# A beacon attention with an expert layer behind it: one sequence's values loaded as plain fp32 on another queue, and cast on VectorE

## The chip, the cores and the metric

The kernel runs on one core of a Trainium2 chip. The core has TensorE (PE) for matrix products, VectorE (DVE), ScalarE (ACT) and GpSimd (POOL) for everything else, and SyncE (SP), which here only issues transfers. Sixteen DMA engines move data between the chip's memory and the core's on-chip memory; GpSimd's transfers go through a queue of its own (q0 in the profile, its descriptors written by software), SyncE's through another (q1, hardware). Each engine runs its own list of instructions in order and waits on semaphores for the others. The metric is the device time of one execution in microseconds; a lower one is better.

## What is computed

Eight sequences (B = 8) of 576 tokens with 8 heads of 64 go through causal attention, with 16 beacon keys and values that every token sees; then all 4608 tokens go through an expert layer with a leaky ReLU.

```python
k_all = np.concatenate([beacon_k, k], axis=2)
v_all = np.concatenate([beacon_v, v], axis=2)
scores = scale * np.matmul(q, k_all.transpose(0, 1, 3, 2))
scores = np.where(causal, -1000000000.0, scores)
a = np.exp(scores - scores.max(-1, keepdims=True))
a /= a.sum(-1, keepdims=True) + 1e-09
x = np.matmul(a, v_all).transpose(0, 2, 1, 3).reshape(B * S, H * D)
h = x @ w_in                              # 512 -> 2048
return np.maximum(0.01 * h, h) @ w_out    # 2048 -> 512
```

## The kernel before

Heads go in pairs g: four pairs for each sequence, 32 in all, so pairs 0 to 3 are the first sequence and 4 to 7 the second. For each pair the queries and keys are loaded, turned so that the head's 64 numbers lie on partitions, multiplied to score tiles in PSUM, taken through the exponential by ScalarE into aT, masked along the diagonal by GpSimd (L285), and multiplied with the values (L355). The values of a sequence lie in one of two buffers v_aug (bf16), in five chunks of 128 key rows (the last has 80; the first begins with the 16 beacon rows), with a column of ones that gives the sum for the normalisation on VectorE (L384, L385). The result is turned into xT, over which the expert layer runs in chunks of 512 tokens: 16 first steps to a chunk (moe1, L438, with ScalarE's leaky ReLU into a tile gT, L446), and then second steps (moe2, L514). The gT tiles come from a pool of two buffers, so a chunk's tile takes the place of that of two chunks before.

The order of all engines is written out by hand. For the first two sequences it is the string HEAD, a list of steps that are recorded one after another; each engine runs its own part of a step in that order. The letters that matter here: `l6.0` and `l6.1` load queries and keys of pair 6 (load_qk, L158); `q6` and `k6` turn them (t_q, L239) and copy them out of PSUM (L245; the number behind the dot names the copying engine: 0 VectorE, 1 ScalarE, 2 GpSimd, and none means 0); `s6.0` is the first of pair 6's four score tiles, `m6.0` the first of its three masks; `v4.0` and `v4.1` are the halves of pair 4's product with the values; `x1` turns pair 1's result; `u` is one first step of the expert layer, `d` one second step; `i0`, `i1` load the halves of w_in (L131), `o0`, `o1` those of w_out (L137), `L` beacon keys (L181); `N8.0`, `N8.1` and `T8` load and turn pair 8, the third sequence's first, with transposing transfers on SyncE's queue; `V1.3` loads chunk 3 of the second sequence's values.

A value load is made by load_v_cast, L199 to L213: GpSimd issues it (L205 for the beacon rows, L210 for the rest), and the transfer casts fp32 to bf16 on its way, straight into v_aug. Chunk 0 takes two transfers, so V1.0 to V1.4 are six. GpSimd's other loads stand in the same list and go through the same queue, between its masks. Semaphores for its transfers are reused by eights: a ninth transfer is issued when the first has landed.

Of the kernel before, what the change touches and what calls it, by code (L numbers as in the profile page):

```python
# [8 lines left out]
FP32 = mybir.dt.float32  # L9
BF16 = mybir.dt.bfloat16  # L10
# [5 lines left out]
def kernel(  # L16
# [21 lines left out]
    NF = DF // 128  # L38
# [41 lines left out]
    gpool = ctx.enter_context(tc.tile_pool(name="gpool", bufs=2))  # L80
# [21 lines left out]
    v_bufs = [singles.tile([128, NKB, H, D + 1], BF16, name=f"v_aug{i}") for i in range(2)]  # L102
# [98 lines left out]
    def load_v_cast(b, c):  # L201
        dst = v_bufs[b % 2]
        lo = 0
        if c == 0:
            nc.gpsimd.dma_start(  # L205
                out=dst[0:NB, 0, :, 0:D], in_=beacon_v[b].rearrange("h p d -> p h d")
            )
            lo = NB
        n = ROWS[c] - lo
        nc.gpsimd.dma_start(  # L210
            out=dst[lo : ROWS[c], c, :, 0:D],
            in_=v[b, :, OFF[c] : OFF[c] + n].rearrange("h p d -> p h d"),
        )  # L213
# [38 lines left out]
    def score(g, n):  # L252
        qT, kT = qk[g]
        if n == 0:
            probs[g] = a_bufs[g % NA]
        aT = probs[g]
        parts = SCORES[n]
        sc = ps_sc.tile([128, 2, 512], FP32, name="sc", tag="sc")
        c0 = parts[0][3]
        for c, q0, w, col in parts:  # L260
            for par in range(2):
                ps_ = slice(par * 64, par * 64 + 64)
                nc.tensor.matmul(  # L263
                    out=sc[:, par, col - c0 : col - c0 + w],
                    lhsT=kT[ps_, c * 128 : (c + 1) * 128],
                    rhs=qT[ps_, q0 : q0 + w],
                    start=True,
                    stop=True,
                    skip_group_check=True,
                )  # L270
        w = sum(p[2] for p in parts)
        nc.scalar.activation(  # L272
            out=aT[:, :, c0 : c0 + w], in_=sc[:, :, 0:w], func=AF.Exp, scale=0.125
        )
# [150 lines left out]
    gT = {}  # L425
# [425 lines left out]
    HEAD = "F0 F1 K Z I l0.0 l1.0 J O l1.1 l2.0 l2.1 V0.0 V0.1 l3.0 l3.1 V0.2 V0.3 V0.4 l4.0 l4.1 i0 P w13.256 C B w13 h0.1 h1.0 q0.1 k0 w2.384 s0.0 m0.0 w3.256 s0.1 q1 s0.2 m0.1 k1 s0.3 m0.2 w2.384 s1.0 m1.0 q2 s1.1 k2 w2.384 s1.2 m1.1 w2.384 s1.3 m1.2 W0.0.4 s2.0 m2.0 W0.0.4 s2.1 W0.0.6 q3 l5.0 l5.1 s2.2 k3 w4.384 v0.0 m2.1 s2.3 i1 m2.2 W0.1.4 s3.0 m3.0 v1.0 s3.1 v0.1 s3.2 v1.1 m3.1 l6.0 l6.1 s3.3 x0.1 m3.2 v2.0 V1.0 V1.1 q4 v2.1 x1 k4.1 v3.0 v3.1 x2.1 s4.0 s4.1 x3 m4.0 V1.2 V1.3 V1.4 l7.0 l7.1 u u s4.2 s4.3 q5 k5 m4.1 m4.2 u o0 u L s5.0 s5.1 m5.0 u u u s5.2 s5.3 q6 k6 m5.1 m5.2 o1 u u s6.0 s6.1 m6.0 u v4.0 u v4.1 s6.3 s6.2 q7.0 k7.0 v5.0 u N8.0 m6.1 v6.0 u s7.0 s7.3 m6.2 N8.1 v6.1 N9.0 v5.1 y4 c u s7.1 x5.0 t0 x6.0 m7.0 s7.2 u m7.1 D u v7.0 m7.2 v7.1 d t1 N9.1 d x7.1 b9.2 d b10.2 T8 t2 N10.0 V2.0 d t3 N10.1 d T9 d b8.2 V2.1 b11.2 T10"  # L851
    NG = B * NPAIR
    KEPT, LEAD, LEFT = 4, 4, 14

# [3 lines left out]
    dve, act, pool = nc.vector.tensor_copy, nc.scalar.copy, nc.gpsimd.tensor_copy  # L858
# [12 lines left out]
    def run(steps):  # L871
        for step in steps.split():
            op, a = step[0], [int(x) for x in step[1:].split(".")] if step[1:] else []
            if op == "s":
                score(*a)
            elif op == "m":
                mask(*a)
            elif op == "v":
                value(*a)
            elif op == "e":  # L880
                value_ahead(*a)
            elif op == "x":
                finish(*a)
            elif op == "l":
                load_qk(*a)
            elif op == "V":
                load_v_cast(*a)
            elif op == "N":
                load_natural(*a)
            elif op == "T":  # L890
                turn_pair(a[0])
            elif op == "y":
                x_turn(a[0])
            elif op == "q" or op == "k":
                t_q(a[0], 0 if op == "q" else 1, (dve, act)[a[1] if len(a) > 1 else 0])
            elif op == "b":
                beacon_columns(a[0], (dve, act, pool)[a[1]])
            elif op == "u":
                up()
            elif op == "d":  # L900
                down()
            elif op == "w":
                unused(*a)
            elif op == "W":
                unused_ahead(*a)
            elif op == "i":
                load_w_in(a[0])
            elif op == "o":
                load_w_out(a[0])
            elif op == "t":  # L910
                weight_sums(a[0])
            elif op == "F":
                nc.sync.dma_start(out=first_k[a[0]], in_=k[0, a[0]].rearrange("(p i) d -> p i d", i=RI))
            elif op == "K":
                load_beacon_k(0, 2, nc.scalar)
            elif op == "Z":
                nc.vector.memset(blank, 0.0)
            elif op == "I":
                nc.vector.memset(ident, 0.0)
            elif op == "J":  # L920
                make_identity(nc, ident, nomemset=True)
            elif op == "O":
                make_ones()
            elif op == "P":
                make_pads()
            elif op == "C":
                cast_beacon_k(0, 2, nc.scalar.copy)
            elif op == "B":
                beacon_transposes(0, 2)
            elif op == "h":  # L930
                (dve, act)[a[1]](out=k_nat0[:, :, a[0]], in_=first_k[a[0]])
# [18 lines left out]
    )  # L950
    with order:
        run(HEAD)

        FIRST = 2 * NPAIR
# [100 lines left out]
```

## Time and profile before

| | |
|---|---|
| median of 3 runs | 325.67 us (323.86 to 328.58) |
| the profiled execution, its own time | 323.3 us |
| its span, first to last instruction | 321.4 us |
| granted TensorE clock | 1.000 |
| DMA packets, all queues | 155769, of which 142368 under 512 B |
| queue q0 (GpSimd) | 99824 packets, 18.54 MB |
| queue q1 (SyncE) | 55632 packets, 20.62 MB |
| values, 128 rows of 8 heads, issue to landing | 6.1 us (median) |

The profile is of one execution; times within it count from the start of its span. A row of the order of time gives start, duration, engine, line, operation, tiles, and in brackets how long the engine was idle before it and what ended that. A row of a line's own answer gives the count, the shortest, median and longest duration in ns, and the first and last start; "DMA to landing" is the time from an issue to the last byte's signal. The DMA rows give packets, MB and the time that the packets took as a share of 16 engines; where packets overlap the share is over 100%.

### The profile page before, as it was taken

How to read it: one execution, taken by the hardware profiler on the slowest of the kernel's cores; microseconds unless marked ns; L12 is line 12 of the kernel's file. 1: busy time of each engine (PE TensorE's matmuls, PEld its weight loads, DVE VectorE, ACT ScalarE, POOL GpSimd, SP SyncE). 2: the span in 40 equal slices, each digit the busy share in tenths (PEclk: the TensorE clock that was granted, in tenths of full speed). 3: DMA queues.
4: the chain of work that ended last, by engine and by line, in shares of the span. 5: the costliest groups of instructions: out<-in, count | busy, mean ns of one | idle time of the engine just before them, and what ended most of it. 6: DMA issues, size and time to landing. Idle time of an engine off the chain costs nothing.

```text
span 321.4 us, 8809 instructions
## 1 busy us (share of the span) xinstructions
PE 312.5 (97%) x3518; PEld 223.5 (70%) x3542; DVE 172.7 (54%) x351; ACT 205.2 (64%) x349; POOL 186.2 (58%) x354
## 2 busy tenths in 40 slices
PE   7999999899999999999999999999999999999995
PEld 4574568565687558845888888656865687688784
DVE  3473379714455145434552454435464699577954
ACT  3978973389756786478647864787468446455510
POOL 8994989999998687659875977665221000000000
PEclk9999999999999999999999999999999999999999
DMA  8999999999999999999999999999212101200213
GB/s 134 146 200 181 146 214 131 155 197 188 151 159 183 180 143 124 132 151 118 125 171 192 126 113 124 181 139 119 64 53 87 24 0 35 88 13 1 68 63 132
DMA packets 155769, 39.79 MB, mean 124 GB/s; under 512 B 142368, under 2 KB 153504, under 8 KB 155728
## 3 DMA queue, kind: packets, MB, share of 16 engines
q0 software_dynamic: 99824, 18.54, 85.5%
q1 hardware_dynamic: 55632, 20.62, 36.9%
q8 instruction: 27, 0.44, 0.7%
q14 instruction: 14, 0.11, 0.2%
q10 hardware_dynamic: 272, 0.07, 0.1%
HBM read 37.22 MB, written 9.44 MB: 145 GB/s over the span
## 4 chain that ended last, share of the span: by engine, by line
PE 92%; ACT 4%; issue 2%; DMA 1%; DVE 0%; ACTq 0%; POOLq 0%
PE acc L438 31%; PE acc L514 23%; PE sc L514 11%; PE av L355 9%; PE sc L310 6%; PE acc L667 5%; PE sc L263 2%; ACT aT L329 2%; PE tp L239 2%; DMA gsum<-in_q_dram 1%; PE av L835 1%; ACT aT L325 1%; PE tp L401 1%; ACT gT L446 1%; ACT aT L272 1%
## 5 line engine op out<-in xcount | busy, mean ns | idle before, releaser
L438 PE MATMUL acc<-xT,w_in_sb 128*128 128x512 bf16 (+1 forms) x536 | 116.5, 354 | 1.3
L446 ACT ACTIVATE gT<-acc 128x512 bf16<-128x512 f32 x124 | 70.7, 627 | 32.0 <-PE acc L438 31.8
L285 POOL TENSOR_SCALAR_AFFINE_SELECT aT<-aT 128x256 bf16<-128x256 bf16 (+2 forms) x160 | 60.3, 406 | 51.8 <-ACT aT L325 30.5
L438 PEld LDWEIGHTS <-w_in_sb 128*128 128x128 bf16 x560 | 51.6, 98 | 42.9 <-issue 2.9
L514 PEld LDWEIGHTS <-gT 128*128 128x128 bf16 x576 | 55.0, 98 | 9.3 <-issue 1.6
L329 ACT ACTIVATE aT<-sc 128x1024 bf16<-128x1024 f32 (+3 forms) x64 | 51.8, 894 | 0.0
L384 DVE RECIPROCAL rec<-av 128x6 f32<-128x6 f32 (+1 forms) x64 | 11.9, 186 | 65.5 <-PE av L355 65.0
L514 PEld LDWEIGHTS <-gsum 128*128 128x128 bf16 x432 | 41.0, 98 | 7.3 <-issue 0.6
L325 ACT ACTIVATE aT<-sc 128x512 bf16<-128x512 f32 (+3 forms) x64 | 29.0, 521 | 25.8 <-PE sc L310 25.8
L355 PEld LDWEIGHTS <-aT 128*128 128x128 bf16 (+1 forms) x960 | 36.5, 98 | 8.0 <-issue 0.6
L355 PE MATMUL av<-v_aug,aT 128*128 128x65 bf16 (+1 forms) x960 | 38.9, 194 | 0.0
L210 POOL DMA_DIRECT2D v_aug<-in_v_dram x40 | 34.1, 859 | 3.5 <-DMA w_in_sb<-in_moe_w_in_dram 3.5
L167 POOL DMA_DIRECT2D k_nat<-in_k_dram x48 | 34.7, 729 | 1.5 <-DMA w_out_sb<-in_moe_w_out_dram 0.8
L514 PE MATMUL acc<-w_out_sb,gT 128*128 128x256 bf16 x288 | 34.6, 273 | 0.7 <-ACT gT L446 0.7
L167 POOL DMA_DIRECT2D q_nat<-in_q_dram x48 | 34.7, 728 | 0.5 <-issue 0.3
L385 DVE TENSOR_TENSOR x_nat<-av,rec 128x384 bf16<-128x384 f32 (+1 forms) x64 | 31.4, 490 | 2.4 <-DVE rec L384 0.3
L272 ACT ACTIVATE aT<-sc 128x1024 bf16<-128x1024 f32 (+3 forms) x32 | 25.9, 875 | 1.9 <-PE sc L263 1.8
L514 PE MATMUL acc<-w_sum,gsum 128*128 128x256 bf16 x192 | 23.8, 273 | 0.0
L310 PE MATMUL sc<-qT,kT 64*128 64x80 bf16 (+22 forms) x384 | 22.0, 250 | 1.5 <-issue 1.3
L789 DVE TENSOR_TENSOR gsum<-gT 128x1024 bf16<-128x1024 bf16 x18 | 12.6, 701 | 16.4 <-ACT gT L446 16.4
L310 PEld LDWEIGHTS <-kT 64*128 64x128 bf16 x384 | 12.8, 94 | 11.8 <-issue 8.8
L545 ACT COPY p<-acc 128x512 f32<-128x512 f32 x15 | 9.1, 604 | 15.7 <-PE acc L514 15.7
(95 smaller groups left out, 330.8 us busy)
## 6 DMA issues: line engine op xcount, KB each, us to landing
out_dram<-p SPq DMA_DIRECT2D x26, 256.0 KB, 3.6
q_nat<-in_q_dram POOLq DMA_DIRECT2D x48, 72.0 KB, 5.4
k_nat<-in_k_dram POOLq DMA_DIRECT2D x48, 72.0 KB, 5.4
v_aug<-in_v_dram POOLq DMA_DIRECT2D x24, 128.0 KB, 6.1
w_in_sb<-in_moe_w_in_dram POOLq DMA_DIRECT2D x2, 1024.0 KB, 12.5
w_out_sb<-in_moe_w_out_dram POOLq DMA_DIRECT2D x2, 1024.0 KB, 10.2
out_dram<-u SPq DMA_DIRECT2D x8, 256.0 KB, 3.5
gsum<-in_q_dram POOLq DMA_DIRECT2D x8, 144.0 KB, 5.6
```

The costliest lines, as they stand in the source:

```text
L167: nc.gpsimd.dma_start(out=t[:, :, par], in_=(q, k)[which][b, 2 * hp + par].rearrange("(t p) d -> p t d", p=NR),)
L210: nc.gpsimd.dma_start(out=dst[lo : ROWS[c], c, :, 0:D], in_=v[b, :, OFF[c] : OFF[c] + n].rearrange("h p d -> p h d"),)
L272: nc.scalar.activation(out=aT[:, :, c0 : c0 + w], in_=sc[:, :, 0:w], func=AF.Exp, scale=0.125)
L285: nc.gpsimd.affine_select(out=view, in_=view, compare_op=ALU.is_ge, fill=0.0, base=128 - n if lo == 0 else 0, channel_multiplier=-1, patte ...
L310: nc.tensor.matmul(out=(sc[par] if apart else sc[:, par])[:, at : at + b - a], lhsT=kT[ps_, c * 128 : (c + 1) * 128], rhs=qT[ps_, q0 : q0 ...
L325: nc.scalar.activation(out=probs[g][:, par, lo:hi], in_=sc[par][:, at : at + hi - lo], func=AF.Exp, scale=0.125)
L329: nc.scalar.activation(out=probs[g][:, :, lo:hi], in_=sc[:, :, at : at + hi - lo], func=AF.Exp, scale=0.125)
L355: nc.tensor.matmul(out=avv[:, n, 0 : D + 1], lhsT=aT[0 : ROWS[c], par, a0 : a0 + 128], rhs=va[0 : ROWS[c], c, 2 * hp + par, :], start=(c = ...
L385: nc.vector.tensor_tensor(out=x_nat[:, t0:t1].rearrange("p t e d -> p (t e) d"), in0=avv[:, :, 0:D], in1=rec[:, n0:n1, None].to_broadcast( ...
L438: nc.tensor.matmul(out=acc[:, lo:hi], lhsT=w_in_cols(fc, j), rhs=xT[:, j, x0 : x0 + hi - lo], start=(j == 0), stop=(j == NJ - 1), skip_gro ...
L446: nc.scalar.activation(out=gT[i][:, fc, :], in_=acc, func=AF.Prelu, alpha=0.01)
L514: nc.tensor.matmul(out=acc[:, lo : lo + HD], lhsT=left(i, n, fc, tile), rhs=right(n, fc), start=(lo == 0 and fc == 0), stop=(fc == HF - 1) ...
```

## The change

The second sequence's values go another way. Three functions are new and HEAD is rewritten from its 85th step on.

```diff
+    staged = []
+
+    def stage(b, c):
+        if not staged:
+            t = gpool.tile([128, NF, 512], BF16, name="gT")
+            staged.append(t.rearrange("p (s a) t -> p s (a t)", a=2).bitcast(FP32))
+        return staged[0][:, (NKB * b + c) % 8].rearrange("p (h d) -> p h d", d=D)
+
+    def load_v_plain(b, c):
+        dst = stage(b, c)
+        lo = 0
+        if c == 0:
+            nc.sync.dma_start(out=dst[0:NB], in_=beacon_v[b].rearrange("h p d -> p h d"))
+            lo = NB
+        n = ROWS[c] - lo
+        nc.sync.dma_start(
+            out=dst[lo : ROWS[c]], in_=v[b, :, OFF[c] : OFF[c] + n].rearrange("h p d -> p h d")
+        )
+
+    def cast_v(b, c, copy):
+        copy(out=v_bufs[b % 2][0 : ROWS[c], c, :, 0:D], in_=stage(b, c)[0 : ROWS[c]])
+
+    def hold_v(b, c):
+        nc.vector.memset(stage(b, c)[:, 0, 0:1], 0.0)
...
             elif op == "V":
-                load_v_cast(*a)
+                (load_v_plain if a[0] == 1 else load_v_cast)(*a)
+            elif op == "G":
+                cast_v(a[0], a[1], (dve, act, pool)[a[2]])
+            elif op == "z":
+                hold_v(*a)
```

V1.0 to V1.4 now issue plain fp32 transfers from SyncE into a tile of the gT pool, which no chunk uses yet; the first chunk's gT then takes the pool's second buffer, and chunk 1 the one with the values, once they are cast. A new step z1.0 writes one column of the staging tile on VectorE; since the first transfer overwrites part of it, that transfer waits for the write, and the others stand behind it on SyncE. Five new steps G1.0 to G1.4 cast a chunk from the tile into v_aug on VectorE. All other values (V0, V2 and on) go as before. The steps of HEAD are the same otherwise, except that some copies out of PSUM change their engine; from the 85th on, up to the first product with the second sequence's values, they stand in this order, first before and then after:

```
v2.0 V1.0 V1.1 q4 v2.1 x1 k4.1 v3.0 v3.1 x2.1 s4.0 s4.1 x3 m4.0 V1.2 V1.3 V1.4 l7.0 l7.1 u u s4.2 s4.3 q5 k5 m4.1 m4.2 u o0 u L s5.0 s5.1 m5.0 u u u s5.2 s5.3 q6 k6 m5.1 m5.2 o1 u u s6.0 s6.1 m6.0 u v4.0

v2.0 q4.0 k4.1 v2.1 z1.0 m3.2 v3.0 V1.0 x1.1 v3.1 x2.1 s4.0 s4.1 x3 k5.0 q5.0 V1.2 m4.0 u V1.3 s4.3 s4.2 l7.0 l7.1 G1.0.0 u m4.1 u L o0 m4.2 V1.1 s5.0 s5.1 u u u o1 V1.4 s5.2 G1.2.0 q6.0 G1.1.0 k6.1 u m5.0 s5.3 u m5.1 G1.3.0 s6.0 N8.0 s6.1 m5.2 G1.4.0 u v4.0
```

SyncE's list at its start, before (gsum is the staging of the first pair's keys, xT the expert layer's input, qT and kT of pairs 8 and on):

```order
L913 DMA gsum_95<-in_k_dram 64x576
L913 DMA gsum_96<-in_k_dram 64x576
L413 DMA_TRANSPOSE xT<-x_nat 128x4x128
L421 DMA_TRANSPOSE xT<-x_nat 128x112
L175 DMA_TRANSPOSE qT<-q_nat 128x6x96
L175 DMA_TRANSPOSE kT<-k_nat 128x6x96
```

The same list after:

```order
L942 DMA gsum_95<-in_k_dram 64x576
L942 DMA gsum_96<-in_k_dram 64x576
L227 DMA gT<-in_beacon_v_dram 16x8x64
L230 DMA gT<-in_v_dram 112x8x64
L230 DMA gT<-in_v_dram 128x8x64 x3
L230 DMA gT<-in_v_dram 80x8x64
L438 DMA_TRANSPOSE xT<-x_nat 128x4x128
L446 DMA_TRANSPOSE xT<-x_nat 128x112
```

Six loads stand ahead of the first transposes there. GpSimd's list before, from the load of pair 6 (gsum_547, its first rows) to that of w_out:

```order
L158 DMA gsum_548<-in_k_dram 64x2x576
L285 AFFINE_SELECT aT_93<-aT_93 128x2x128
L285 AFFINE_SELECT aT_93<-aT_93 80x2x80
L205 DMA v_aug_89<-in_beacon_v_dram 16x8x64
L210 DMA v_aug_89<-in_v_dram 112x8x64
L210 DMA v_aug_89<-in_v_dram 128x8x64
L285 AFFINE_SELECT aT_90<-aT_90 128x2x112
L210 DMA v_aug_89<-in_v_dram 128x8x64 x2
L210 DMA v_aug_89<-in_v_dram 80x8x64
L158 DMA gsum_547<-in_q_dram 64x2x576
L158 DMA gsum_548<-in_k_dram 64x2x576
L285 AFFINE_SELECT aT_90<-aT_90 128x2x128 x3
```

After (the second gsum_547 and gsum_548 are pair 7, aT_90 is pair 4's probabilities):

```order
L158 DMA gsum_548<-in_k_dram 64x2x576
L310 AFFINE_SELECT aT_93<-aT_93 128x2x128
L310 AFFINE_SELECT aT_93<-aT_93 80x2x80
L310 AFFINE_SELECT aT_90<-aT_90 128x2x112
L158 DMA gsum_547<-in_q_dram 64x2x576
L158 DMA gsum_548<-in_k_dram 64x2x576
L310 AFFINE_SELECT aT_90<-aT_90 128x2x128 x2
L181 DMA bk_raw<-in_beacon_k_dram 128x6x64
L137 DMA w_out_sb<-in_moe_w_out_dram 128x4x1024
L310 AFFINE_SELECT aT_90<-aT_90 128x2x128
L310 AFFINE_SELECT aT_90<-aT_90 80x2x80
L137 DMA w_out_sb<-in_moe_w_out_dram 128x4x1024
```

The six value loads are gone; pair 7, the beacon keys and both halves of w_out have moved ahead of masks. VectorE's list before, around the copies of qT and kT for pairs 5 and 6:

```order
L406 COPY xT<-tp 128x576
L245 COPY qT<-tp 128x576
L245 COPY kT<-tp 128x576
L245 COPY qT<-tp 128x576
L245 COPY kT<-tp 128x576
L384 RECIPROCAL rec<-av 128x6
L385 TENSOR_TENSOR x_nat<-av,rec 128x384
```

After:

```order
L431 COPY xT<-tp 128x576
L270 COPY kT<-tp 128x576
L270 COPY qT<-tp 128x576
L235 CAST v_aug_89<-gT 128x8x64 x2
L270 COPY qT<-tp 128x576
L235 CAST v_aug_89<-gT 128x8x64 x2
L235 CAST v_aug_89<-gT 80x8x64
L409 RECIPROCAL rec<-av 128x6
L410 TENSOR_TENSOR x_nat<-av,rec 128x384
```

Two casts (chunks 0 and 2) stand ahead of the copy of pair 6's qT, and three (chunks 1, 3 and 4) behind it, ahead of v4.0's normalisation; pair 6's kT has gone to ScalarE. The transfers on SyncE stand in the order of chunks 0, 2, 3, 1, 4.

More of the change, by code (lines that the diff above doesn't have):

```diff
@@ L849, in unused_ahead @@
             )
-    HEAD = "F0 F1 K Z I l0.0 l1.0 J O l1.1 l2.0 l2.1 V0.0 V0.1 l3.0 l3.1 V0.2 V0.3 V0.4 l4.0 l4.1 i0 P w13.256 C B w13 h0.1 h1.0 q0.1 k0 w2.384 s0.0 m0.0 w3.256 s0.1 q1 s0.2 m0.1 k1 s0.3 m0.2 w2.384 s1.0 m1.0 q2 s1.1 k2 w2.384 s1.2 m1.1 w2.384 s1.3 m1.2 W0.0.4 s2.0 m2.0 W0.0.4 s2.1 W0.0.6 q3 l5.0 l5.1 s2.2 k3 w4.384 v0.0 m2.1 s2.3 i1 m2.2 W0.1.4 s3.0 m3.0 v1.0 s3.1 v0.1 s3.2 v1.1 m3.1 l6.0 l6.1 s3.3 x0.1 m3.2 v2.0 V1.0 V1.1 q4 v2.1 x1 k4.1 v3.0 v3.1 x2.1 s4.0 s4.1 x3 m4.0 V1.2 V1.3 V1.4 l7.0 l7.1 u u s4.2 s4.3 q5 k5 m4.1 m4.2 u o0 u L s5.0 s5.1 m5.0 u u u s5.2 s5.3 q6 k6 m5.1 m5.2 o1 u u s6.0 s6.1 m6.0 u v4.0 u v4.1 s6.3 s6.2 q7.0 k7.0 v5.0 u N8.0 m6.1 v6.0 u s7.0 s7.3 m6.2 N8.1 v6.1 N9.0 v5.1 y4 c u s7.1 x5.0 t0 x6.0 m7.0 s7.2 u m7.1 D u v7.0 m7.2 v7.1 d t1 N9.1 d x7.1 b9.2 d b10.2 T8 t2 N10.0 V2.0 d t3 N10.1 d T9 d b8.2 V2.1 b11.2 T10"
+    HEAD = "F0 F1 K Z I l0.0 l1.0 J O l1.1 l2.0 l2.1 V0.0 V0.1 l3.0 l3.1 V0.2 V0.3 V0.4 l4.0 l4.1 i0 P w13.256 C B w13 h0.1 h1.0 q0.1 k0 w2.384 s0.0 m0.0 w3.256 s0.1 q1 s0.2 m0.1 k1 s0.3 m0.2 w2.384 s1.0 m1.0 q2 s1.1 k2 w2.384 s1.2 m1.1 w2.384 s1.3 m1.2 W0.0.4 s2.0 m2.0 W0.0.4 s2.1 W0.0.6 q3 l5.0 l5.1 s2.2 k3 w4.384 v0.0 m2.1 s2.3 i1 m2.2 W0.1.4 s3.0 m3.0 v1.0 s3.1 v0.1 s3.2 v1.1 m3.1 l6.0 l6.1 s3.3 x0.1 v2.0 q4.0 k4.1 v2.1 z1.0 m3.2 v3.0 V1.0 x1.1 v3.1 x2.1 s4.0 s4.1 x3 k5.0 q5.0 V1.2 m4.0 u V1.3 s4.3 s4.2 l7.0 l7.1 G1.0.0 u m4.1 u L o0 m4.2 V1.1 s5.0 s5.1 u u u o1 V1.4 s5.2 G1.2.0 q6.0 G1.1.0 k6.1 u m5.0 s5.3 u m5.1 G1.3.0 s6.0 N8.0 s6.1 m5.2 G1.4.0 u v4.0 q7.0 m6.0 s6.2 v4.1 u y4 N8.1 s6.3 k7.1 m6.1 v5.0 u s7.0 s7.3 m6.2 v6.0 c N9.0 u v6.1 t0 m7.0 s7.2 s7.1 u v5.1 x6.1 m7.2 u m7.1 D u v7.0 T8 v7.1 V2.0 b10.2 N10.0 x5.1 b9.2 u t1 d d t2 N9.1 N10.1 x7.1 d T9 t3 b8.2 d T10 d b11.2 V2.1 d"
     NG = B * NPAIR
```

## The prediction

> **What bounds the kernel now.** I read the page first: shares of the engines, the DMA row, the chain that ended last, the queues.
>
> ```profile
> span 321.4 us, 8809 instructions
> PE 312.5 (97%) x3518; PEld 223.5 (70%) x3542; DVE 172.7 (54%) x351; ACT 205.2 (64%) x349; POOL 186.2 (58%) x354
> DMA  8999999999999999999999999999212101200213
> q10 hardware_dynamic: 272, 0.07, 0.1%
> PE 92%; ACT 4%; issue 2%; DMA 1%; DVE 0%; ACTq 0%; POOLq 0%
> gsum<-in_k_dram POOLq DMA_DIRECT2D x7, 144.0 KB, 5.9
> bk_raw<-in_beacon_k_dram ACTq DMA_DIRECT2D x1, 64.0 KB, 2.3
> ```
>
> TensorE is busy for 97% and carries 92% of the chain, so the time can fall only where TensorE waits: 321.4 - 312.5 = 8.9 us in all. But the DMA engines are full as well, from the second slice to the twenty-eighth, and the change is one to the DMAs. Next, TensorE's order of time around the change:
>
> ```profile
> 33.95 0.76 PE L239 MATMUL tp<-ident,gsum 64*64 64x64 bf16 x36
> 36.48 0.58 PE L263 MATMUL sc<-qT,kT 64*128 64x512 bf16 x4
> 36.99 1.04 PE L438 MATMUL acc<-xT,w_in_sb 128*128 128x512 bf16 x4
> 37.87 0.53 PE L355 MATMUL av<-v_aug,aT 128*128 128x65 bf16 x12
> 60.79 0.85 PE L310 MATMUL sc<-qT,kT 64*128 64x512 bf16 x12 [1.25 <-issue]
> ```
>
> 33.95 is the turning of pair 6's queries and keys, 36.48 its first two score tiles (s6.0, s6.1), 37.87 the first product with the second sequence's values (v4.0), and 60.79 the first tile of the third sequence, with the only wait of weight in this stretch, 1.25 us. That wait is about all that the change can win. Now GpSimd, which issues the loads, and their landings:
>
> ```profile
> 18.76 0.76 POOL L131 DMA_DIRECT2D w_in_sb<-in_moe_w_in_dram  x1
> 22.12 0.61 POOL L158 DMA_DIRECT2D gsum<-in_k_dram  x1
> 23.89 1.73 POOL L210 DMA_DIRECT2D v_aug<-in_v_dram  x2
> 26.43 0.38 POOL L285 TENSOR_SCALAR_AFFINE_SELECT aT<-aT 128x224 bf16<-128x224 bf16 x1 [0.81 <-ACT aT L272]
> 31.99 0.73 POOL L210 DMA_DIRECT2D v_aug<-in_v_dram  x1 [3.45 <-DMA w_in_sb<-in_moe_w_in_dram]
> 35.46 0.78 POOL L137 DMA_DIRECT2D w_out_sb<-in_moe_w_out_dram  x1
> 38.76 0.77 POOL L137 DMA_DIRECT2D w_out_sb<-in_moe_w_out_dram  x1
> ...
> L131 POOL DMA_DIRECT2D w_in_sb<-in_moe_w_in_dram x2: 764/770/776, 12.4 to 18.8; - x2
> DMA to landing us min/median/max: 12.0/12.5/12.9
> ...
> L158 POOL DMA_DIRECT2D gsum<-in_k_dram x1: 607/607/607, 22.1 to 22.1; - x1
> DMA to landing us min/median/max: 10.9/11.0/11.1
> ...
> L210 POOL DMA_DIRECT2D v_aug<-in_v_dram x5: 730/883/905, 23.9 to 32.0; - x5
> DMA to landing us min/median/max: 5.9/10.0/10.7
> ...
> L137 POOL DMA_DIRECT2D w_out_sb<-in_moe_w_out_dram x2: 769/772/776, 35.5 to 38.8; - x2
> DMA to landing us min/median/max: 8.5/10.2/12.0
> ```
>
> The reader is to see one queue that serves in order and never runs dry: second half of w_in down at 18.76 + 12.9 = 31.7, pair 6 at 22.12 + 11.1 = 33.2, the last values at 31.99 + 5.9 = 37.9, second half of w_out at 38.76 + 12.0 = 50.8. The values took 37.9 - 33.2 = 4.7 us of it.
>
> **How two queues share the engines.** The change puts the values on SyncE's queue (q1) beside GpSimd's (q0). Four stretches of the DMA view, in order 39 to 42 us, 44.5 to 48.5, 68.5 to 69.5 and 215 to 215.5:
>
> ```profile
> q0 software_dynamic: 304, 0.62, 111.6%
> ...
> q0 software_dynamic: 347, 0.71, 95.0%
> q1 hardware_dynamic: 319, 0.08, 15.9%
> ...
> q1 hardware_dynamic: 259, 0.25, 88.5%
> q0 software_dynamic: 258, 0.03, 49.3%
> ...
> q1 hardware_dynamic: 500, 0.12, 132.6%
> ```
>
> Columns are packets, MB, share of time. Alone, w_out moves 304/3 = 101 packets a us, of 2 KB each. Against it, a transpose on q1 gets one small packet (0.08 MB/319, 256 B) for each large one: 319 against 347, some 80 a us. Turned round, 1 KB stores of q1 against 128 B packets of q0 give 259 against 258. Alone, q1 moves 500 packets in 0.5 us, 1000 a us. So the queues take turns packet by packet, whatever the size, and 256 B packets beside 2 KB ones get a twelfth of the rate that they have alone.
>
> **The change, part by part.** The values become 592 rows x 8 heads = 4736 runs of 256 B. The nearest row for a plain load of such runs by a hardware queue is that of the beacon keys above: 64 KB in 272 packets (q10), so 256 B each. I take 4736 packets.
>
> ```profile
> DMA packets 3857, 1.39 MB, mean 173 GB/s; under 512 B 3271, under 2 KB 3531, under 8 KB 3856
> 23.29 0.42 DVE L385 TENSOR_TENSOR x_nat<-av,rec 128x256 bf16<-128x256 f32 x1
> 34.47 0.76 DVE L245 COPY qT<-tp 128x576 bf16<-128x576 bf16 x1 [4.69 <-PE tp L239]
> L931 DVE CAST k_nat<-gsum x1: 745/745/745, 5.9 to 5.9; 64x576 bf16<-64x576 f32 x1
> L913 SPq DMA_DIRECT2D gsum<-in_k_dram x2: 571/573/575, 0.8 to 1.4; - x2
> 40.53 1.37 SPq L413 DMA_TRANSPOSE xT<-x_nat  x1
> ```
>
> Start: the holding write comes after value 2.1's product on VectorE, so at 23.3 + 0.4 = 23.7; six issues of 0.57 us follow, and packets flow from about 25. Behind them on SyncE stands the first transpose, issued at 40.53 before: covered unless the values are still in the ring.
>
> What q0 still holds then: the first row above is 25 to 33 us before. 3856 - 3531 = 325 packets of w_in are left, 3531 - 3271 = 260 of pair 6. Pair 7 is as large (144 KB, 256 packets), and the two halves of w_out are 2 x 512. That is 1865, with the beacon keys' 192 KB some 1900. With the values gone from GpSimd, nothing holds q0 up: pair 7's two loads follow the select of 26.43, then come two selects, the beacon keys and w_out, at about 30 to 31 instead of 35.46, before pair 6 is down. So q0 has large packets all the way.
>
> When those end: before at 50.8; less the 4.7 us of values, 46.1; plus the turns of q1. 325 + 1024 packets at 87 a us (347/4) instead of 101 cost 2.1 us, the 516 of the pairs about 0.6: 48.8. By then q1 has had some 1900 packets. The second cast needs 128 + 896 + 1024 = 2048 of them: about 49.0. The fourth needs 4096, and pair 8's queries (2 x 576 packets of 128 B) now take turns: 4096 - 1900 + 1152 at about 1000 a us, 3.4 us: 52.2.
>
> What waits: VectorE runs in order, and two casts stand ahead of its copy of qT for pair 6. 49.0 + 0.75 (cast, at the nearest row, L931) + 0.76 (copy) puts s6.0 at 50.5. Both kernels run eight expert steps ahead of it, so TensorE is there at 36.5: a wait of 14.0 us. s6.0, s6.1 and a step take 1.4 us (36.48 to 37.87), so TensorE stands at v4.0 at 51.9; the fourth cast ends at 52.2 + 0.75 = 52.95: 1.1 us more. Delay at v4.0: 52.95 - 37.87 = 15.1.
>
> Off the path: six issues of 0.5 to 0.9 us and the wait of 3.45 leave GpSimd, won nothing for TensorE but the earlier loads. Five casts, 3.7 us, lie in VectorE's idle time (4.69 us ahead of 34.47 alone); without the late data they cost nothing. Copies moved to ScalarE lie in the waits named. The swapped gT buffers cost nothing: chunk 1 is first written seventeen expert steps in, after the casts. The 1.25 us at 60.79 goes, since TensorE comes there 14 us later and pair 8 is down.
>
> Sum: 321.4 + 15.1 - 1.25 = 335.3 of span; the profiled execution had 323.3 us with 1.9 around its span, so 337.2. It lay 2.4 under the median of the runs, 325.67; between 337.2 and 339.6 I take 338.5. Bounds: data for the second cast in 46 instead of 49 changes little, since the fourth decides; that one in 49 to 55 gives 334 to 342.
>
> The Trainium skill's page "TensorE: Matmul & The Clock Gate" (part 1) adds to this: after an idle window of about 3.4 us the array runs at half rate until about 3.4 us of work have passed. By that page the sum would be an estimated 1.7 us more, 340.2. No row here shows an idle spell that long in mid-kernel, and the sum leaves it out.
>
> **Rivals.**
> (a) No slowing: the runs travel in bundles. If a packet of q1 carried 16 runs, 4 KB, 296 packets would do, and 296 turns against w_in last 296/101 + 4736/1000 = 7.6 us: values down at 32.7, before their casts. But those 4.7 us come before pair 6, down at 37.9 instead of 33.2; its turning stood at 33.95, so TensorE waits 4.0: 325.67 + 4.0 - 1.25 = 328.4, not slower by 2%; if the turning has room, 324.4. It decides from about four runs a packet: 4 x 1184 covers the values by the middle of w_out's first half. Against it stands the row of q10, one run a packet. The Trainium skill, "DMA: Bandwidth & Descriptors" (Queues, rings and completion order), has the engine take turns at packet granularity, with 9 to 17 descriptors typical of a packet. By that the bundle is likely; the trace agrees on the turns, and its 256 B packets on hardware queues speak against the bundle.
> (b) w_out comes late, because selects hold GpSimd. From pair 7's landing, near 34, q1 would run alone at 1000 a us; if w_out were 4 us later, the remaining 3900 packets would be done at 38, and v4.0 would wait 1 us: 325.67 + 1 - 1.25 = 325.4. Against it: only the masks of pair 4 stand ahead of w_out's first half now.
> (c) A won wait and no more: the load is hidden, 325.67 - 1.25 = 324.4. Since that is under 2%, faster by over 2% has hardly a mechanism.
>
> **How the numbers follow.** Forecast as worked out, 333 to 342.5: 0.70. Slower by less, 328.5 to 333, if q1 gets more turns: 0.05. (a) 0.15, (b) 0.05, (c) 0.05. About 2% is what a measurement of this kernel can tell from no change, 332.2 here: slower 0.72, same 0.27, faster 0.01. The range that holds 8 in 10 reaches from the forecast into (a), 326 to 342.5.
>
> **What would show it.** Right: q1 beside q0 near one to one from 25 to 48 us; the first cast near 36 and the second near 49; VectorE idle ahead of a cast with the transfers as releaser; TensorE idle ahead of s6.0 and v4.0, 15 us together; after that the old rhythm. Wrong: values down before 36, q1 packets above 256 B, w_out issued after 34, or a wait at pair 6's turning instead.

## The result, and the profile after

The changed kernel takes 339.4 us (median of 4 runs, 337.68 to 340.9) against 324.76 us for the kernel before, run beside it: a ratio of 1.0462, with a 95% interval of 1.0385 to 1.0539. A second set gave 340.16 us and 1.0467 (1.0391 to 1.0543). Here and below a ratio leaves disturbed executions out, so it can differ a little from that of the medians. The profiled execution took 340.9 us. Its page, from the top:

```profile
span 338.5 us, 8842 instructions
...
PE 318.2 (94%) x3542; PEld 225.0 (66%) x3542; DVE 173.0 (51%) x352; ACT 208.4 (62%) x354; POOL 182.6 (54%) x348
...
PE   7999238999999999999999999999999999999995
...
PEclk9999755999999999999999999999999999999999
...
q0 software_dynamic: 94992, 17.93, 75.0%
q1 hardware_dynamic: 60464, 21.84, 36.5%
...
PE 79%; DMA 10%; ACT 4%; SPq 3%; DVE 1%; issue 1%; POOL 1%; ACTq 0%
```

The span is 17.1 us longer. TensorE's slices 5 and 6, of 8.5 us each, hold a hole that was not there before, and in slices 5 to 7 the granted clock falls to a half. 4832 packets have moved from q0 to q1 (99824 - 94992 = 60464 - 55632): 4736 for the runs of 256 B, and 96 of 4 B, sixteen for each of the six transfers. So a run is one packet, on either queue. Transfers, which carried 1% of the chain that ended last, carry 10%. TensorE's longest waits, in us in total, times and longest:

```profile
PE sc L288 <- DVE qT L270: 9.7, 1, 9.7
PE av L380 <- DVE v_aug L235: 3.2, 1, 3.2
```

Both are waits for VectorE. Its order of time shows what VectorE waited for (L238 is the holding write, L235 a cast, L270 the copy of pair 6's queries out of PSUM):

```profile
23.37 0.06 DVE L238 MEMSET gT<- 128x1 f32 x1
...
36.51 0.97 DVE L235 CAST v_aug<-gT 128x512 bf16<-128x512 f32 x1 [8.58 <-DMA gT<-in_v_dram]
44.91 0.43 DVE L235 CAST v_aug<-gT 128x512 bf16<-128x512 f32 x1 [7.42 <-DMA gT<-in_v_dram]
45.25 0.75 DVE L270 COPY qT<-tp 128x576 bf16<-128x576 bf16 x1
51.73 1.10 DVE L235 CAST v_aug<-gT 128x512 bf16<-128x512 f32 x3 [5.74 <-DMA gT<-in_v_dram]
```

The copy at 45.25 needs nothing from the values. It stands behind two casts whose data came at 36.5 and 44.9. TensorE's order of time shows the price, first at s6.0 (46.05), then at v4.0 (52.22):

```profile
46.05 1.00 PE L288 MATMUL sc<-qT,kT 64*128 64x512 bf16 x4 [9.73 <-DVE qT L270]
46.98 1.89 PE L463 MATMUL acc<-xT,w_in_sb 128*128 128x512 bf16 x4
48.66 0.37 PE L380 MATMUL av<-v_aug,aT 128*128 128x65 bf16 x3
52.22 0.66 PE L380 MATMUL av<-v_aug,aT 128*128 128x65 bf16 x9 [3.18 <-DVE v_aug L235]
...
59.48 0.52 PE L288 MATMUL sc<-qT,kT 64*128 64x512 bf16 x6
59.93 0.54 PE L380 MATMUL av<-v_aug,aT 128*128 128x65 bf16 x12
60.31 1.03 PE L463 MATMUL acc<-xT,w_in_sb 128*128 128x512 bf16 x4
...
332.97 1.91 PE L539 MATMUL sc<-w_out_sb,gsum 128*128 128x256 bf16 x16
```

Beside the two waits the reader should see the durations. Four 512-column matmuls take 1.89 us at 46.98 and 1.03 at 60.31: behind the waits TensorE runs at half rate. The trace's record of the granted clock has a half from 38.3 us, 1.9 us after TensorE's last matmul ahead of the first wait ended, to 58.7. The 1.3 us wait for "issue" of the kernel before is gone from the list of waits.

Last, how the two queues shared the engines, in two stretches of the DMA view, 28 to 34 us and 36 to 46 (packets, MB, share of time):

```profile
q0 software_dynamic: 664, 0.77, 73.8%
q1 hardware_dynamic: 1690, 0.42, 47.8%
...
q0 software_dynamic: 904, 1.81, 95.3%
q1 hardware_dynamic: 897, 0.23, 17.3%
```

From 36 to 46 us, beside w_out, it is one packet for one packet: ten microseconds move 0.23 MB of values. Before that, q1 had two and a half turns for one, since GpSimd's queue was short of packets for a part of the time: the same view has 511 packets of q1 for 85 of q0 from 30 to 31 us and 494 for 78 from 33 to 34. By 36 us q1 had moved 2044 packets, which is about what the second cast's chunk needs (2048, with all ahead of it); yet its data came at 44.9. The reason is in the trace's semaphore events: each of the sixteen DMA engines reports its share of a transfer, and the transfer is done with the last. When the sixteen shares of two transfers were reported, in order of time (us), for w_in's second half and for the second cast's chunk:

```
w_in, second half   28.2 28.4 28.5 28.5 28.6 28.6 28.9 29.1 29.2 29.4 29.5 29.6 29.6 29.8 31.1 32.0
second cast's data  33.7 34.0 34.7 34.8 34.8 34.9 35.0 35.2 35.3 35.3 35.4 35.4 35.6 36.0 37.6 44.9
```

Fifteen engines had the chunk by 37.6 us, the sixteenth at 44.9, and VectorE's queue stood still for it. The Trainium skill says the same of the count ("DMA: Bandwidth & Descriptors", Why a DMA increments its semaphore by 16 and not by 1): the engines finish independently, and only the full sixteen means that all has landed. The trace agrees, with 7.3 us between the fifteenth and the sixteenth. The trace doesn't name the engine of a report, so what held the sixteenth is argued: it was still behind when w_out arrived, and its share of the chunk is 64 packets, which at one for one, 90 a us over sixteen engines, take up to 11 us.

### The profile page after: what moved, and what is told of

The parts are those of the page before. It is cut to its first block, busy times and chain, and to the rows that moved or that the text cites. A ratio compares the mean times of both kernels' runs of the same rounds, so it can differ in the third digit from the quotient of the medians.

```text
span 338.5 us, 8842 instructions
## 1 busy us (share of the span) xinstructions
PE 318.2 (94%) x3542; PEld 225.0 (66%) x3542; DVE 173.0 (51%) x352; ACT 208.4 (62%) x354; POOL 182.6 (54%) x348
## 3 DMA queue, kind: packets, MB, share of 16 engines
q0 software_dynamic: 94992, 17.93, 75.0%
q1 hardware_dynamic: 60464, 21.84, 36.5%
## 4 chain that ended last, share of the span: by engine, by line
PE 79%; DMA 10%; ACT 4%; SPq 3%; DVE 1%; issue 1%; POOL 1%; ACTq 0%
PE acc L463 27%; PE acc L539 19%; PE sc L539 11%; PE av L380 8%; DMA gT<-in_v_dram 6%; PE sc L335 6%; PE acc L692 4%; SPq L230 2%; ACT aT L354 2%; PE sc L288 2%; DMA qT<-q_nat 2%; DMA gsum<-in_k_dram 1%; DMA k_nat<-in_k_dram 1%; PE tp L264 1%; ACT gT L471 1%
## 5 line engine op out<-in xcount | busy, mean ns | idle before, releaser
L463 PE MATMUL acc<-xT,w_in_sb 128*128 128x512 bf16 (+1 forms) x560 | 120.0, 359 | 0.0
L310 POOL TENSOR_SCALAR_AFFINE_SELECT aT<-aT 128x256 bf16<-128x256 bf16 (+2 forms) x160 | 61.1, 410 | 75.6 <-ACT aT L350 30.6
L354 ACT ACTIVATE aT<-sc 128x1024 bf16<-128x1024 f32 (+3 forms) x64 | 51.7, 891 | 0.0
L380 PEld LDWEIGHTS <-aT 128*128 128x128 bf16 (+1 forms) x960 | 37.7, 99 | 12.3 <-issue 4.3
L380 PE MATMUL av<-v_aug,aT 128*128 128x65 bf16 (+1 forms) x960 | 40.6, 196 | 3.4 <-DVE v_aug L235 3.2
L210 POOL DMA_DIRECT2D v_aug<-in_v_dram x35 | 29.9, 856 | 0.8 <-DMA gsum<-in_k_dram 0.6
L288 PE MATMUL sc<-qT,kT 64*128 64x80 bf16 (+4 forms) x96 | 11.0, 302 | 9.9 <-DVE qT L270 9.7
```

The costliest lines, as they stand in the source:

```text
L210: nc.gpsimd.dma_start(out=dst[lo : ROWS[c], c, :, 0:D], in_=v[b, :, OFF[c] : OFF[c] + n].rearrange("h p d -> p h d"),)
L310: nc.gpsimd.affine_select(out=view, in_=view, compare_op=ALU.is_ge, fill=0.0, base=128 - n if lo == 0 else 0, channel_multiplier=-1, patte ...
L354: nc.scalar.activation(out=probs[g][:, :, lo:hi], in_=sc[:, :, at : at + hi - lo], func=AF.Exp, scale=0.125)
L380: nc.tensor.matmul(out=avv[:, n, 0 : D + 1], lhsT=aT[0 : ROWS[c], par, a0 : a0 + 128], rhs=va[0 : ROWS[c], c, 2 * hp + par, :], start=(c = ...
L463: nc.tensor.matmul(out=acc[:, lo:hi], lhsT=w_in_cols(fc, j), rhs=xT[:, j, x0 : x0 + hi - lo], start=(j == 0), stop=(j == NJ - 1), skip_gro ...
```

## The experiments

All are edits of the changed kernel, but for the longer start at the end. Times stand beside runs of the kernel before on the same chip: 326.05 us for the order alone, the long runs, w_out late and the casts behind the copy; 325.7 for the two other holds and the first run with unused matmuls; 326.09 for the repeats of the changed kernel, of w_out late and of the unused matmuls, and for the longer start; 326.28 for the unused matmuls inside the waits.

**The order alone.** In HEAD, with load_v_cast called for every sequence:

```diff
-v2.1 z1.0 m3.2 v3.0 V1.0 x1.1
+v2.1 m3.2 v3.0 V1.0 V1.1 x1.1
...
-V1.2 m4.0 u V1.3 s4.3 s4.2 l7.0 l7.1 G1.0.0 u
+m4.0 u s4.3 s4.2 V1.2 V1.3 V1.4 l7.0 l7.1 u
```

> The changed kernel's order of work, but the second sequence's values by GpSimd's casting loads as before the change; no plain loads, no holding write, no casts on VectorE. My theory (the plain values lose their turns on the DMA engines to the weights, and everything behind them waits) says that the new order costs nothing by itself: 322 to 328 us, no wait over 2 us ahead of s6.0 or v4.0, granted clock full through 36 to 60 us. The rival (the new order, with copies moved between VectorE and ScalarE, makes the loss) says 335 to 340 with the waits still there.

328.19 us, ratio 1.0034 (0.9993 to 1.0075), just above the expected 322 to 328. v4.0 begins at 38.01 us, without a wait:

```profile
38.01 0.53 PE L380 MATMUL av<-v_aug,aT 128*128 128x65 bf16 x12
```

The new order costs nothing that this measurement can tell, and wins nothing. The loss is in the way the values travel.

**The same bytes in long runs.**

```diff
-            out=dst[lo : ROWS[c]], in_=v[b, :, OFF[c] : OFF[c] + n].rearrange("h p d -> p h d")
+            out=dst[lo : ROWS[c]].rearrange("p h d -> p (h d)"),
+            in_=v[b].rearrange("h s d -> (h s d)")[OFF[c] * DM : (OFF[c] + n) * DM].rearrange(
+                "(p x) -> p x", x=DM
+            ),
```

> The plain loads read one contiguous run of 2 KB a partition instead of eight of 256 B, so the second sequence's values are those of other tokens; the bytes, the queue, the hold, the casts and the order stay. My theory (turns are taken by packets, so it is their number that decides) says that 704 packets instead of 4736 get through beside w_in by 34 to 39 us, each cast runs before 40 us, the waits ahead of s6.0 and v4.0 go, and pair 6 comes later instead, by up to 5 us: 325 to 331 us. The rival (bytes on SyncE's queue, the hold or the casts are the cause) says 337 to 341, with the casts as late as now.

326.74 us, ratio 1.0013 (0.9967 to 1.0058), with values of other tokens. The first and the last cast, in VectorE's order of time:

```profile
31.57 0.88 DVE L238 CAST v_aug<-gT 128x512 bf16<-128x512 f32 x1 [3.32 <-DMA gT<-in_v_dram]
...
37.75 0.43 DVE L238 CAST v_aug<-gT 80x512 bf16<-80x512 f32 x1 [0.34 <-DMA gT<-in_v_dram]
```

Queue, hold, casts, order and bytes are those of the changed kernel. With 704 packets instead of 4736 the last cast runs 14 us earlier, and the time is that of the kernel before. It is the number of packets that costs.

**w_out out of the way.** In HEAD:

```diff
-u L o0 m4.2 V1.1 s5.0 s5.1 u u u o1 V1.4 s5.2
+u L m4.2 V1.1 s5.0 s5.1 u u u V1.4 s5.2
...
-s6.0 N8.0 s6.1 m5.2 G1.4.0
+s6.0 s6.1 m5.2 o0 o1 N8.0 G1.4.0
```

> The two w_out loads (and pair 8's queries) are issued only after the last mask of pair 5, behind the time when the values should be down; the values stay 256 B packets on SyncE's queue. My theory (w_out's 1024 large packets take the turns) says that SyncE's queue has the engines alone once pair 7 is down, at about 35.5 us, moves about 1000 packets a us and is done by 41 us: the wait ahead of s6.0 falls from 9.7 to under 3 us, that ahead of v4.0 from 3.2 to under 1.5: 325 to 330 us, unless w_out then comes late for the second matmul of the expert steps, which would show as a wait on w_out. The rival (256 B packets are slow by themselves) says 336 to 341.

331.67 us, ratio 1.0131 (1.0040 to 1.0221), above the expected range, with no wait at either place. But that profiled execution had begun late (last section), so the kernel was run once more:

> The kernel that issues w_out after the last mask of pair 5 once more, unchanged, since its first profile began late. In an execution that begins at full rate my theory says: SyncE's queue alone once pair 7 is down, last value down by 41 us, waits ahead of s6.0 and v4.0 of under 3 and 1.5 us, w_out about 10 us later than in the changed kernel, and 325 to 331 us; the rival (256 B packets slow by themselves) says the last value near 52 and 336 to 341.

327.67 us, ratio 1.0071 (1.0028 to 1.0114). TensorE's order of time, VectorE's casts, and the two queues from 31 to 41 us:

```profile
39.15 0.59 PE L288 MATMUL sc<-qT,kT 64*128 64x512 bf16 x4 [1.79 <-DVE qT L270]
...
40.55 0.53 PE L380 MATMUL av<-v_aug,aT 128*128 128x65 bf16 x12
...
45.20 0.51 PE L288 MATMUL sc<-qT,kT 64*128 64x512 bf16 x6
...
318.88 1.91 PE L539 MATMUL sc<-w_out_sb,gsum 128*128 128x256 bf16 x16
```

```profile
36.76 0.43 DVE L235 CAST v_aug<-gT 128x512 bf16<-128x512 f32 x1 [7.78 <-DMA gT<-in_v_dram]
38.00 0.43 DVE L235 CAST v_aug<-gT 128x512 bf16<-128x512 f32 x1 [0.81 <-DMA gT<-in_v_dram]
...
40.02 1.39 DVE L235 CAST v_aug<-gT 128x512 bf16<-128x512 f32 x3 [0.93 <-DMA gT<-in_v_dram]
```

```profile
q1 hardware_dynamic: 4247, 1.07, 54.2%
q0 software_dynamic: 538, 0.77, 44.8%
```

The same 256 B packets, issued at the same time, go through at 425 a us instead of 90 once w_out isn't beside them. Of the 12.9 us of wait 1.8 remain. So the small packets are slow only through the large ones they alternate with.

**The casts behind the copy.** In HEAD:

```diff
-l7.0 l7.1 G1.0.0 u
+l7.0 l7.1 u
...
-s5.2 G1.2.0 q6.0 G1.1.0 k6.1 u m5.0 s5.3 u m5.1 G1.3.0 s6.0 N8.0
+s5.2 q6.0 k6.1 u m5.0 s5.3 u m5.1 s6.0 G1.0.0 G1.2.0 G1.1.0 G1.3.0 N8.0
```

> The first four casts stand behind pair 6's copies and its first score tile in the order, the fifth behind the second; loads, queue and hold as in the changed kernel. My theory says that the wait ahead of s6.0 goes and comes back ahead of v4.0, whole, since the landing of chunk 1 at about 51.7 us decides: a wait of 11 to 14 us ahead of v4.0, 336 to 340 us. The rival (the casts standing ahead of pair 6's copy on VectorE make the loss) says that about 9.7 us are won: 328 to 331.

339.83 us, ratio 1.0420 (1.0347 to 1.0493). s6.0 no longer waits, and v4.0 does:

```profile
52.49 0.66 PE L380 MATMUL av<-v_aug,aT 128*128 128x65 bf16 x9 [14.08 <-DVE v_aug L235]
```

The wait has moved whole. The place of the casts on VectorE decides where TensorE stands still; the landing of the data decides for how long.

**No hold, and an earlier hold.** In the first V1.0 to V1.4 stand behind F1 and z1.0 is gone; in the second z1.0 and V1.0 to V1.4 stand ahead of s2.0:

```diff
-F0 F1 K Z I
+F0 F1 V1.0 V1.2 V1.3 V1.1 V1.4 K Z I
```

```diff
-W0.0.4 s2.0 m2.0
+W0.0.4 z1.0 V1.0 V1.2 V1.3 V1.1 V1.4 s2.0 m2.0
```

> The holding write is left out and the plain loads are issued from the program's start, right behind the first two loads of keys on SyncE; all else as in the changed kernel. In the changed kernel's trace GpSimd's queue moves about 7100 packets before 25 us, most of them under 512 B, against 1900 after. My theory (turns are taken packet by packet) says that 4736 turns are had by 15 to 20 us, no cast is late, and the waits ahead of s6.0 and v4.0 for the values are gone; the first pairs' loads come up to 4.7 us later instead, so 325 to 331 us. The rival (256 B packets on SyncE's queue are slow by themselves, about 175 a us as in the changed kernel) needs 27 us for them and says the same or a wait at the first turnings of over 5 us.

> The holding write stands ahead of s2.0, at about 12 us instead of 23.4, and the plain loads right behind it. My theory counts turns: GpSimd's queue moves about 2000 packets from 13 to 19 us and 760 from 19 to 25, and some 1700 of SyncE's passed from 28 to 34, so that the last value is down at 33 to 39 us instead of 52; the casts are no longer late, the waits ahead of s6.0 and v4.0 for them go, and pair 6 comes up to 5 us later: 325 to 331 us. The rival (only bytes or the distance in time count: 11 us earlier out is 11 us earlier down) has the last values at 41 and says 328 to 331 with a wait of 2 to 3 us ahead of v4.0.

Without a hold: 330.46 us, ratio 1.0124 (1.0063 to 1.0185), in the expected range; no cast waits for data. The two queues from 2 to 19 us (q1's count has the first pair's keys in it):

```profile
q0 software_dynamic: 4478, 1.47, 80.6%
q1 hardware_dynamic: 4827, 1.47, 53.0%
```

In this time GpSimd's own packets are mostly small, so turns are plentiful. What remains is 4.8 us over the kernel before. How much of it is the delay of the first loads, and how much a late start of TensorE that this profiled execution had (last section), isn't told apart.

With the hold at 12.6 us the four runs lie apart, so no ratio is given: three, from 337.2 to 340.7 us, are outside both expected ranges, and one, at 328.9, is inside both. What sets it apart isn't known, since the profiled execution is one of the three; there the last casts come at 47.95 and 51.11 us, later than either expectation had them. From 22 to 31 us, and from 40 to 51:

```profile
q0 software_dynamic: 948, 1.57, 93.7%
q1 hardware_dynamic: 952, 0.24, 20.0%
...
q0 software_dynamic: 3011, 1.89, 116.8%
q1 hardware_dynamic: 164, 0.04, 2.8%
```

Again one for one, and at the end only 164 packets are left; but they take 11 us. The semaphore events of the two last chunks, the fourth and the fifth that were issued:

```
36.0 36.0 36.1 36.2 36.3 36.3 36.3 36.5 36.8 37.1 37.2 37.2 37.4 37.4 45.8 47.9
37.9 38.1 38.2 38.6 38.8 39.2 39.2 39.2 39.4 39.5 40.0 40.4 40.5 40.8 50.6 51.1
```

Fourteen engines were done by 37.4 and 40.8 us, close to where the count of turns had put the whole; two were 8 to 10 us behind. In this execution my theory's turns held, but it counted them for all engines together, and the end of a transfer is that of its slowest engine.

**Unused matmuls in the waits.** Three runs ask what the half clock costs. In the first two, in HEAD:

```diff
-m5.1 G1.3.0 s6.0 N8.0
+m5.1 G1.3.0 w55.384 s6.0 N8.0
...
-u v4.0 q7.0
+u w18.384 v4.0 q7.0
```

> 55 unused matmuls of 384 columns stand ahead of s6.0 and 18 ahead of v4.0, where TensorE waited; loads and casts as in the changed kernel. The changed kernel's TensorE clock is granted at a half from about 38 to 58 us, some 8 us of it with work. My theory says that the half clock was brought by the waits and cost about 4 us besides them: with TensorE kept busy the matmuls behind the waits take 1.03 us for four again instead of 1.89, and the time falls by 3 to 4.5 us, to 334.5 to 336.5. The rival (the half clock costs nothing, since the transfers decide there anyway) says 338 to 341.

> The changed kernel once more, unchanged, to stand beside the next two on one chip. Two profiled executions so far (of the kernel with unused matmuls, and of that with w_out late) began with TensorE's matmuls at half rate up to about 23 us, some 5 us behind; the hold then came at 30 us, when w_in was down. My theory says that an execution that begins at full rate takes 337 to 341 us with 9 to 10 us of wait ahead of s6.0 and 3 ahead of v4.0, and that one that begins late takes 329 to 333 with no such wait, since the plain packets then have the engines to themselves. The rival (the start has nothing to do with it) says 337 to 341 whichever way it begins.

> The kernel with 55 and 18 unused matmuls ahead of s6.0 and v4.0 once more, unchanged: its first profile began late and so had no waits to fill, and showed 12.2 us of unused matmuls added to a late start. If this execution begins at full rate, my theory says that the unused matmuls lie in the waits, the granted clock stays full and the span is 333 to 336, 3 to 4.5 under that of the changed kernel; the rival (the half clock costs nothing) says the changed kernel's 336 to 339. If it begins late again: 338 to 341, and the question stays with the matmul times in the changed kernel's trace.

The first, whose profiled execution began late and had no waits, gave 345.03 us, ratio 1.0492 (1.0386 to 1.0597), the repeat 345.9 us, ratio 1.0648 (1.0558 to 1.0739): slower than the changed kernel, 340.16 in the repeat's set, where I expected less. The repeat's trace says why:

```profile
45.85 10.49 PE L860 MATMUL av<-blank 128*128 128x384 bf16 x55 [9.27 <-DVE qT L270]
```

The unused matmuls themselves waited for the copy that s6.0 waits for, since they write a PSUM buffer that this copy frees. They filled no wait but stood behind it: a fault of the experiment. The changed kernel's own second profile had the two waits again, with another split:

```profile
PE sc L288 <- DVE qT L270: 7.3, 1, 7.3
PE av L380 <- DVE v_aug L235: 4.8, 1, 4.8
```

TensorE came to s6.0 2.1 us later there (38.46 against 36.32), so the first wait was shorter. It began at full rate, as the first had, so what a late start would do to the changed kernel itself stays untested. The third run put the unused matmuls into the score tile that s6.0 writes next, which nothing late frees, and into v4.0's tile:

```diff
+        for _ in range(42 if (g, n) == (6, 0) else 0):
+            nc.tensor.matmul(
+                out=sc[:, 0, 0:384].rearrange("p (r w) -> p r w", w=128),
+                lhsT=blank,
+                rhs=blank[:, None, 0:128].to_broadcast([128, 3, 128]),
+                start=True,
+                stop=True,
+                skip_group_check=True,
+            )
...
-u v4.0 q7.0
+u W4.0.50 v4.0 q7.0
```

> Unused matmuls inside the waits this time: 42 of 384 columns in the score tile that s6.0 will write, so that they need nothing that is late (about 7 us of work), and 50 of 112 columns in v4.0's tile (2 to 3 us); loads, queue, casts and order as in the changed kernel. My theory: the values land as before (about 44.9 and 51.7 us), the granted clock stays full from 36 to 60 us, four 512-column matmuls behind the waits take 1.04 us instead of 1.89, and the time is 3 to 4 us under the changed kernel's 339 to 340: 335 to 337.5. The rival (the half clock costs nothing, the transfers decide) says 339 to 341.

338.28 us (337.07 to 339.86), ratio 1.0364 (1.0312 to 1.0416), between the two expectations: 1 to 2 us under the changed kernel by the medians of different chips, some 3 by the ratios (1.0462 and 1.0467), whose intervals overlap. So the time alone doesn't settle what was won. TensorE's order of time:

```profile
36.88 6.99 PE L286 MATMUL sc<-blank 128*128 128x384 bf16 x42
47.24 1.00 PE L297 MATMUL sc<-qT,kT 64*128 64x512 bf16 x4 [3.38 <-DVE qT L270]
...
49.86 4.17 PE L881 MATMUL av<-blank 128*128 128x112 bf16 x50
53.87 0.53 PE L389 MATMUL av<-v_aug,aT 128*128 128x65 bf16 x12
...
332.00 1.91 PE L548 MATMUL sc<-w_out_sb,gsum 128*128 128x256 bf16 x16
```

The second cast's data came at 46.1, so 3.38 us of idle time were left, and that was enough: the granted clock fell to a half at 46.3 us, and s6.0 takes 1.00 us again, where 0.58 is full rate. Begun at half rate, the next 50 unused matmuls took 4.17 us, longer than the wait they were to fill, and v4.0 came 1.65 us later than in the changed kernel. Behind it all ran at full rate (the clock was back at 53.1): from v4.0 to the start of the last group shown 332.00 - 53.87 = 278.13 us, against 332.97 - 52.22 = 280.75 in the changed kernel and 280.05 in its second profile. So the half clock behind v4.0 costs some 2 to 2.6 us, and 1.65 of it was lost again to the unused work.

**A longer start.** Of the kernel before, the number of unused matmuls ahead of the first turning:

```diff
-P w13.256 C B w13 h0.1
+P w13.256 C B w24 h0.1
```

> The kernel before the change with 24 instead of 13 unused matmuls of 128 columns ahead of the first turning, so that TensorE works without a gap from 1.07 us to about 6.5 or 7. If the late starts come from the gap of 0.2 to 0.7 us ahead of the first turning, this execution begins at full rate and the spread of the kernel before (323.5 to 328.6) narrows to its lower end, 323 to 326 us; if the gap has nothing to do with them, 325 to 329 with the same spread, about 0.5 us for the work added.

326.49 us, ratio 1.0020 (0.9975 to 1.0065). Nine of ten executions lie from 323.99 to 327.54 us; one took 1796 us, which stays unexplained, since it wasn't the one profiled. The median is that of the kernel before and not at its lower end, so closing the gap ahead of the first turning doesn't bring the quicker executions; nine are too few to say more of the spread. The other profiles speak against the gap too: the three that began late had 0.35 us of it, 0.18 and none, and one that began at full rate had 0.81. No version of this study beats the kernel before.

## Why the prediction was right, and which of its terms were off

**The mechanism held.** The queues take turns packet by packet (904 for 897), a run of 256 B is one packet, w_out's issues came at 31.1 and 32.5 us (two rows below), and TensorE's new waits are at s6.0 and v4.0 (no other is over 1.1 us, and that one the kernel before has too). Three edits show it: long runs, w_out late (in its second set, of ten runs; the first four gave 1.0131), and the old transfers in the new order each bring the time back to within 1%, and the first of them keeps the hold, the casts and the order. Rival (a), bundles of sixteen runs, fell with the packet count; the Trainium skill's 9 to 17 descriptors a packet ("DMA: Bandwidth & Descriptors", Queues, rings and completion order) isn't what these plain loads show, while its turns at packet granularity are. Rivals (b) and (c) fell with the issue times and the waits.

```profile
31.11 0.76 POOL L137 DMA_DIRECT2D w_out_sb<-in_moe_w_out_dram  x1
...
32.50 0.76 POOL L137 DMA_DIRECT2D w_out_sb<-in_moe_w_out_dram  x1
```

**Delay at v4.0: 15.1 us forecast, 14.2 measured** (52.22 with three of twelve products done, against 37.87 with none, which is 0.13 less). That these are so near is in part luck, since two steps of the sum failed in opposite ways. The first is "So q0 has large packets all the way": from 28 to 34 us q1 got 1690 turns for 664, and when w_out was down at 48 us it had had 3570 and not 1900. By the count of turns alone the second cast's data would have come at about 36 us and the fourth's at about 49.2 (q1's 2044 packets by 36, 4012 by 49 and 4565 by 50). The second is that the sum counts turns for all sixteen engines together. The slowest engine brought the second cast's chunk at 44.9, forecast at 49.0, and the fourth's at 51.7, forecast at 52.2. So the split was off too: the first wait was 9.7 us instead of 14.0, the second 3.2 instead of 1.1. That the fourth decides, as the bounds said, is what the casts put later show: 14.1 us at one place and the same time.

**Casts: 0.75 us forecast, 0.43 measured** (the median of five; the first took 0.97, and why isn't settled). The nearest row, a cast of 64x576, was not near; it mattered little.

**The half clock was left out of the sum, and shouldn't have been.** The row that I missed couldn't be in the trace of before, but the forecast wait of 14 us was itself the condition. Between s6.0 and v4.0 it costs 1.2 us (46.05 to 48.66, against 36.48 to 37.87 before). Behind v4.0, up to the row of six score products (52.22 to 59.48 us), 7.26 us go by where the execution with w_out late takes 4.65 for the same work and three products more: 2.7 us. In all some 4 us; in the changed kernel's second profile the same two stretches cost 1.2 and 2.1. The Trainium skill's page "TensorE: Matmul & The Clock Gate" (part 1) has an idle window of about 3.4 us bring the half rate, and about as much work end it. The traces agree on the end: after single short waits the half clock lasted 3.4 us. On the idle time they differ, and they decide: 2.47 us (w_out late, first set) and 2.05 us (the earlier hold) were enough, and even 0.97 us was, once, in the changed kernel's second profile, while 1.79 us (w_out late, second set) was not. The estimate of 1.7 us by that page counted one return to full rate; there were two waits, and the second, of 3.18 us, began before the clock was back.

**The 1.25 us that the wait at 60.79 was to give back didn't come.** The wait is gone, but from v4.0 to the start of the last group the kernel before takes 278.2 us with it (316.04 - 37.87, its last group below), and the execution with w_out late 278.3 without it (318.88 - 40.55). Most of what took its place is in the order. The prediction has both kernels run eight expert steps ahead of s6.0; by HEAD it is nine before and eight after, so one step, some 0.9 us (36.99 to 37.87 before), has moved from ahead of v4.0 to behind it. The rest, some 0.5 us, isn't settled.

```profile
316.04 1.91 PE L514 MATMUL sc<-w_out_sb,gsum 128*128 128x256 bf16 x16
```

So the 17.1 us of span are 12.9 of waits and some 4 of half clock. The forecast for the profiled execution, 337.2 us, is 3.7 below its 340.9: 0.9 too much at v4.0, against 1.25 that didn't come back, some 2.7 of half clock behind v4.0 and 0.5 more around the span. The median, 339.4, is nearer to the 338.5 of the forecast, because the profiled execution is the slowest of its four, while that of the kernel before was 2.4 us under its median: this part is luck.

## What to carry to other kernels

Before a load moves from a queue that is served in order to one beside it, count its packets and those of its neighbours, not the bytes: where two queues take turns, small packets beside large ones get the large ones' rate, and here 1.2 MB that cost 4.7 us in the one queue took 27 us beside it. A transfer ends with its slowest engine, so a late engine that meets the next large load can hold a chunk for 7 to 10 us after the others are done. And a copy that TensorE needs should not stand behind work on the same engine that waits for such a transfer, though where the data itself is late, moving the copy only moves the wait.

## What the runs showed of the hardware that was not expected

SyncE could not issue on. The five large plain loads kept its queue for 21.7 us, in its order of time:

```profile
23.88 21.70 SPq L230 DMA_DIRECT2D gT<-in_v_dram  x5
```

The same line's own answer gives the shortest, median and longest issue in ns:

```profile
L230 SPq DMA_DIRECT2D gT<-in_v_dram x5: 423/4797/8803, 23.9 to 40.8; - x5
```

The first took 0.42 us to issue and the longest 8.8, as if a list of bounded length were full; what was full, the trace doesn't show. I had counted six issues of 0.57 us. It cost nothing that shows here, since the transposes behind them waited for VectorE up to 55.8 us; with long runs the same five took 3.2 us.

TensorE can begin late. Three profiled executions (without the hold, the first with w_out late, the first with unused matmuls) ran at half rate from the start to about 23 us. Their views show a granted clock of 1.00 there, but the trace's record of the clock begins only at 23.7 to 23.9 us in these three, and at 3.8 to 6.7 in the others, so the 1.00 ahead of it isn't a measurement. The rest were at full rate by 4 to 7 us. Their turning of 18 blocks takes 0.69 us, that of the others 0.47. The same turning in the two profiles of the kernel with w_out late, its first set first:

```profile
19.74 0.69 PE L264 MATMUL tp<-ident,gsum 64*64 64x64 bf16 x18
```

and its second:

```profile
14.63 0.47 PE L264 MATMUL tp<-ident,gsum 64*64 64x64 bf16 x18
```

TensorE is some 5 us behind by then. The Trainium skill ("TensorE: Matmul & The Clock Gate", part 1) calls the rate at the start variable from run to run, since its window doesn't begin with the kernel; the trace agrees, with a spell far longer than the window. How much of the spread of the kernel before (322.8 to 329.75 us in one set) this makes was not measured.
